# A hand-ordered attention and feed-forward kernel on one core: an earlier bias load, a warm-up on ones and another written-out order

## The chip, the core and the metric

The kernel runs on one core of one Trainium2 chip. The engines of the core run side by side, each through its own queue of instructions in order: TensorE (PE, with its weight loads PEld), VectorE (DVE), ScalarE (ACT), GpSimd (POOL) and SyncE (SP), which here only issues DMAs and passes signals on. DMAs of SP and ACT go over the hardware queues, those of POOL over the software queue. The metric is the device time of one execution in microseconds (us). Three runs of the kernel before took 156.56, 155.41 and 156.89 us; their median is 156.56 us.

## The reference

The input x has 2048 tokens of 448 features, in bf16. It is layer-normed, and the normed xn goes two ways.

```
xn = (x - mean) / sqrt(var + 1e-5)
A: q, k, v = xn @ wqkv, 16 heads of 28
   token s attends to the 8 tokens s, s-2, ..., s-14 (those below 0 are masked)
   s  = softmax(q.k / sqrt(28)) v, heads joined, @ wo
B: h = gelu(xn @ w1 + b1)          (1792 wide)
   g = silu(h @ w2 + b2)
out = x + s * g
```

## The kernel before, in words

Even and odd tokens never attend to each other, so the tokens are sorted into two halves, and 16 tiles of 128 tokens are worked on. For each tile DVE takes the statistics (lines 340 and 344), normalises (line 374) and doubles the last 64 features (line 379), so that the contraction of 448 is three k tiles of 128 rows and one of 64 that is there twice. Tiles 0 to 3 are transposed by PE (line 389) and copied out of PSUM; all later tiles by DMA transposes on SP (line 287).

Most products come as a **pair** (lines 412 to 436): two products run in the upper and lower 64 rows of PE side by side, first part one (4 steps each), then a **hop**, an empty instruction on POOL or SP (line 424) that waits for part one's end and lets part two (3 steps each) start on exchanged rows. The pairs make q, k and v (lines 465 and 489), the first feed-forward product in four chunks of 512 tokens (line 524, with the gelu and the bias b1 in line 528 on ACT), the second one (line 550, 14 and 14 steps) and the output product (line 732). q and k go back through SBUF and SP's DMA transposes to qkT, v through POOL's DMAs (line 281). The attention is 9 blocks of scores (line 650), exp (line 660), mask (line 666), values (line 682) and four DVE steps (lines 692 to 706). Rows that have to change place between the halves are moved by SP's DMAs (lines 627 and 633). The last four tiles use whole products (lines 576 and 747).

Each of the 1044 steps is a task with a number, the engines that it may run on, its dependences and the buffers that it takes and gives back. **ORDER** (lines 17 to 63) is a string that lists all tasks; the letter says the engine: P for PE, V for DVE, A for ACT, G for POOL, S for SP; D is the landing of a DMA. `emit` (line 99) walks through it, so it fixes the order within every queue, and which buffer a task gets: the one of its ring that was given back first. The eight PSUM banks are such a ring.

Tasks that the prediction speaks of, with what they are:

- G17 the identity; G100, G102 and G104 the three masks (one memset and four or six selects each, lines 795 to 802); G50 the memset and G51/D52 the load of b1 as rows (b1r); P190 (line 836) its transpose on PE.
- V1 the memset of the warm-up operand (line 250) and P2 to P14 the 13 warm-up products (line 253).
- P132 to P137 (line 446) the first products of tiles 0 and 1 by k tile, P138 (line 453) their last 64 rows; P122 and P123 the transposes of tile 2, V120 and V121 its normalisation; P128 and P129, V126 and V127 the same of tile 3; V130 the copy of tile 3's transpose.
- P326 and P321 the first feed-forward pairs; they need all of tiles 0 to 3 and the first half of w1.
- P621, hop G622 and P623: the first pair of the second feed-forward product; V627 adds b2 to one of its two results (line 592) and gives back a bank; G280/D281 the load of b2 to all partitions.
- P241 and P234: part one of the pairs that make v of tiles 6 and 7, and q and k of tile 7; P386 the same for tile 10.
- V427 and V428 the normalisation of tile 12, S429/D430 its DMA transpose, P443 part one of its q and k.
- P450, hop 451, P452: q and k of tile 13.
- S232/D233 the transpose of tile 6's q and k, P747 the scores that need them, P374 part one of tile 9's pair and S375/G375 its hop, S441 the transpose of tile 15.
- A54 the load of ACT's table for gelu.

Of the kernel before, what the change touches and what calls it, by code (L numbers as in the profile page):

```python
# [14 lines left out]


ORDER = """
D0 V1 G17 G104 S34 D35 A36 D37 V15 P2 V16 V22 S38 D39 V23 V24 G50 V25 V26 V27 P3 S44 D45 V28 V29 V30 G51 D52 V18 V19
P4 V20 S40 D41 V21 G31 P5 S42 D43 A53 G32 P6 G33 S46 D47 P7 V60 S48 D49 P8 V61 V64 P9 A62 S76 D77 G100 P10 V63 P11
P12 V106 S78 D79 P13 P14 V107 P108 S80 D81 V65 P109 A66 V110 A111 V67 P132 V113 D112 G102 S82 D83 V114 P115 P136  # L20
V117 V68 S86 D87 P116 P133 A118 V69 P190 D119 P137 A70 V71 S88 D89 V120 P134 V121 V72 S90 D91 P122 P123 P135 V73
V191 V124 A74 P138 V75 D125 V126 P149 A139 V127 V140 A143 P128 G150 P129 A148 A54 S141 D142 P151 V130 G168 D169 D131
P326 V153 G170 D171 G172 D173 V101 P163 V84 A145 G327 G174 D175 A152 V96 P328 G178 D179 A144 S154 D155 V85 V97 G176
D177 V94 P156 A329 G164 V95 V92 P321 A330 G99 P165 G322 P341 V200 A167 V204 A166 V205 V201 P323 A325 V93 G342 G157
S202 D203 G98 V192 P331 G332 P343 A324 P158 S206 D207 A344 A345 G180 D181 V196 V193 S194 D195 P333 A334 P346 P316
A159 V197 G182 D183 S198 D199 A335 P336 G317 S272 D273 G337 G347 A160 P318 A319 P348 A350 A349 P227 G228 V298 P338
A340 P229 V230 A339 V302 S276 D277 S278 D279 G252 D253 P222 S274 D275 A320 G280 D281 G223 P536 G537 P224 A231 P538
A539 P526 V304 V305 V225 P546 S146 D147 P215 G184 D185 V300 G527 A540 A226 P516 P528 A529 V301 V299 S232 D233 S161
D162 V303 G306 V351 V363 G547 P548 G517 P518 A530 A519 V103 G290 D291 G216 P217 A218 V359 A520 P521 G522 P541 G542
A550 P523 V355 V356 V219 S357 D358 A524 P531 V313 S220 D221 V307 P543 V364 P208 A549 G186 D187 G532 A545 G286 D287  # L30
V360 P533 A534 G209 P210 A535 A211 A212 A525 A544 A55 V352 P621 P693 V311 A698 A696 S365 D366 A700 V309 V310 G622
P623 V314 V308 V312 G315 V431 A694 S361 D362 V627 V435 P711 A718 A712 P234 G235 V105 V701 V699 P241 A716 G242 V697
V717 G246 D247 S353 D354 P236 S213 D214 G248 D249 P243 G855 A714 V624 G256 D257 A237 P386 V436 V695 P702 V703 V704
S387 P388 A244 G284 D285 A389 A390 A238 V439 V440 G288 D289 V705 G264 D265 G260 D261 V715 V707 V708 A245 G250 D251
V719 P630 G266 D267 G258 D259 S239 D240 V427 G188 D189 V706 V428 S631 S429 D430 P729 A625 A730 A734 V626 P632 A732
G254 D255 V636 S437 D438 V735 A736 A637 V638 G296 D297 V737 G268 D269 V633 P374 G375 P367 S391 D392 G368 P376 A377
P369 P443 A370 G444 A371 S372 D373 V713 V709 P720 V710 V731 A628 V629 P445 A378 V733 A446 A447 G282 D283 P639 V725
V721 V432 A634 S640 V722 S441 D442 V723 V724 V635 S873 D874 P747 A754 A748 V726 V727 V728 S433 D434 P641 V642 S379
D380 V645 P393 G394 A752 G856 S865 D866 P738 V749 G294 D295 P395 V739 V743 V740 P400 S401 A750 P381 G409 D410 G382
A397 P402 V396 G262 D263 V741 V742 S857 D858 P469 V744 G405 D406 G470 S448 D449 S883 D884 P383 A403 V745 A385 S869  # L40
D870 S875 D876 G270 D271 V746 P457 G458 A404 A384 V755 P471 G413 D414 S871 D872 V473 A472 P459 S398 D399 S887 D888
A461 V460 P765 A768 A770 V769 P476 A772 V751 A766 P450 G477 P478 V753 S451 P452 P756 G482 D483 G415 D416 A479 V480
V454 S863 D864 G498 D499 S474 D475 G292 D293 S889 D890 S877 D878 A453 V773 V771 V761 P783 A786 V762 G407 D408 S891
D892 V757 S881 D882 G417 D418 S455 D456 A788 G419 D420 G423 D424 A784 P648 S649 A643 A790 A56 G504 D505 V758 S885
D886 P581 G582 P462 S463 V759 V767 A646 V647 G484 D485 V763 V764 P583 A585 V644 V760 S893 D894 P650 A584 P464 V651
A652 V787 S879 D880 V654 A466 A655 G411 D412 P774 V779 V775 V780 P571 V789 G488 D489 V776 G572 A465 V781 P556 P576
V777 V778 P573 A574 S859 D860 G577 S861 D862 V782 A575 P578 A580 S557 V656 S867 D868 P558 A579 P551 G552 P566 P553
A555 A554 S567 V785 A560 P964 S903 D904 S965 G425 D426 S897 D898 S467 D468 V791 P568 G494 D495 G496 D497 A570 P966
G421 D422 A569 P953 V967 V968 A559 P561 S562 V971 S969 D970 G954 P955 V972 S973 D974 S899 D900 V956 V960 P563 A565
A564 A57 V957 P792 V793 V797 V794 G481 S895 D896 V795 P801 A806 S901 D902 P657 S658 V796 V798 V807 V961 A802 S962  # L50
D963 A808 S911 D912 S905 D906 V653 A804 V805 S907 D908 V799 P819 A822 V803 V800 S913 D914 G490 D491 A824 V825 G500
D501 G486 D487 P659 G492 D493 A826 V809 V660 S915 D916 S909 D910 A661 P810 V811 G510 D511 V815 A820 V663 A664 P666
P837 A840 V816 V817 S667 V812 V813 V814 A838 P668 S919 D920 A844 P986 V818 P975 V665 V672 G514 D515 G502 D503 G987
S923 D924 V662 P988 V989 S976 P977 S929 D930 V993 S958 D959 V990 V669 A842 A58 S925 D926 V994 S991 D992 S931 G506
D507 D932 A670 P591 A673 V982 P586 S587 S921 D922 V978 G592 P593 V841 V823 G508 D509 V821 S917 D918 V979 V827 P596
S597 A594 A595 S927 D928 V839 P588 A590 A589 P598 A600 P616 P828 V833 V834 V835 S617 P618 A599 A619 S980 D981 V836
P611 V983 P1008 A620 V843 S612 P613 P601 A614 V829 V830 V831 S995 D996 S1009 P1010 G602 P603 S984 D985 A615 V832
S933 D934 P997 S998 P606 S607 V674 V1015 A605 V1011 V1016 S1017 D1018 P999 P608 V845 G512 D513 P846 A604 P679 S941
D942 V1012 S1013 D1014 V1000 S939 D940 S937 D938 A609 V847 V851 A610 A59 V848 V852 V849 V853 S935 D936 V850 V854
S943 D944 V671 V1001 S1002 D1003 V1004 S951 D952 S945 D946 S949 D950 S947 D948 V1005 P687 P675 P676 V677 A678 P688  # L60
P1019 P680 V1020 V681 V1021 P1024 S1022 D1023 A682 V1025 V1026 A689 S1006 D1007 S1027 D1028 P683 P684 P1034 V685
A686 P1029 V1035 V1036 S1037 D1038 V1030 P690 P691 V1031 A692 S1032 D1033 P1039 V1040 V1041 S1042 D1043
"""


# [58 lines left out]
def kernel(  # L124
# [106 lines left out]
    plan = _Plan()  # L231
# [11 lines left out]
    def memset(eng, ap, v):  # L243
        def fn(_):
            getattr(nc, eng).memset(ap, v)
        return fn

    warm = p_h.bufs[-1]
    t_on = plan.add("DMA", lambda _: None, ())
    t_warm = plan.add("DVE", memset("vector", warm[:], 0.0), [t_on])  # L250
    for n in (512,) * 8 + (P,) * 5:
        def idle(k, n=n):
            nc.tensor.matmul(buf(p_b, k)[:, :n], warm[:, :P], warm[:, :n], start=True, stop=True)
        t_warm = plan.add("PE", idle, [t_warm], take=(p_b,))
# [669 lines left out]
```

## Time and profile before

| | us |
|---|---|
| runs, median (lowest to highest) | 156.56 (155.41 to 156.89) |
| the profiled execution's own time | 156.29 |
| its span, first to last instruction | 154.5 |
| outside the span | 1.8 |
| PE busy / DVE / ACT / POOL | 147.0 / 105.3 / 89.9 / 45.3 |

The span holds 5764 instructions. In a view, "idle before" is the time that an engine stood still in front of a group, and "<-" names who ended it. The end of a product is modelled, as PE overlaps them; the distance from start to start of two groups is therefore the safer measure of what PE needs for one. A pair's part one on 448 columns takes 0.757 us from start to start, part two 0.567; on 512 columns 0.865 and 0.649. The landing of a DMA is the last of the marks that it leaves on its semaphore.

### The profile page before, as it was taken

To read this page: it belongs to the slowest core of one execution; us is meant where nothing else is said; L and a number is where in the kernel's file an instruction comes from. 1 tells how busy PE (TensorE), PEld (TensorE's weight loads), DVE (VectorE), ACT (ScalarE), POOL (GpSimd) and SP (SyncE) were. 2 spreads that over 40 slices of the span, in tenths; PEclk is the share of its full clock that TensorE was granted. 3 is DMA by queue.
4 is the path that set the end of the run, shared out by engine and by line. 5 is a ranking of instruction groups with operands and counts; after the bars stand their busy time and mean duration, and the time that the engine had idled before them with its cause. 6 is when DMAs were issued, how large, how long until landed. Compare 5 with 4: busy or idle time off the path is not lost.

```text
span 154.5 us, 5764 instructions
## 1 busy us (share of the span) xinstructions
PE 147.0 (95%) x2404; PEld 80.0 (52%) x2404; DVE 105.3 (68%) x271; ACT 89.9 (58%) x167; POOL 45.3 (29%) x100
## 2 busy tenths in 40 slices
PE   6679999999999999899999999999999999999990
PEld 2335555555565555455555445447655565455560
DVE  4967720655503695996978589539987796999462
ACT  3228677847698655634276944696837186660310
POOL 6834650241302495010534821148000110100000
PEclk9999999999999999999999999999999999999999
DMA  5999936999773049642689662055100111121022
GB/s 155 305 286 319 178 92 134 378 290 213 153 75 60 17 110 152 112 98 50 140 158 139 121 75 80 0 129 145 55 17 14 52 55 55 50 71 38 12 89 62
DMA packets 35442, 18.29 MB, mean 118 GB/s; under 512 B 25643, under 2 KB 34263, under 8 KB 35416
## 3 DMA queue, kind: packets, MB, share of 16 engines
q1 hardware_dynamic: 33208, 14.92, 44.2%
q0 software_dynamic: 2064, 2.88, 8.7%
q8 instruction: 19, 0.31, 0.8%
q10 hardware_dynamic: 144, 0.11, 0.3%
q14 instruction: 7, 0.06, 0.2%
HBM read 7.69 MB, written 2.10 MB: 63 GB/s over the span
## 4 chain that ended last, share of the span: by engine, by line
PE 84%; DMA 7%; DVE 4%; POOL 2%; issue 1%; POOLq 0%; DVEq 0%; SPq 0%
PE bank L524 28%; PE bank L550 18%; PE bank L465 11%; PE bank L489 7%; PE bank L576 7%; PE bank L732 5%; PE bank L682 4%; DMA b1r<-in_B_b_dram 4%; DMA xnT<-xn 4%; PE bank L650 3%; PE bank L747 1%; DVE sg L755 1%; DVE dt L692 1%; POOL m L802 0%; POOL m L800 0%
## 5 line engine op out<-in xcount | busy, mean ns | idle before, releaser
L524 PE MATMUL bank<-xnT,w 64*128 64x512 bf16 x392 | 46.3, 376 | 0.0
L281 POOL DMA_DIRECT2D v<-v_tok x52 | 27.4, 533 | 62.5 <-PE bank L732 23.8
L528 ACT ACTIVATE h<-bank,b 128x512 bf16<-128x512 f32 x56 | 35.1, 687 | 16.4 <-PE bank L524 16.1
L550 PE MATMUL bank<-w,h 64*128 64x448 bf16 x336 | 33.9, 349 | 0.0
L524 PEld LDWEIGHTS <-w 64*128 64x128 bf16 x392 | 21.4, 94 | 19.3 <-issue 0.3
L465 PE MATMUL bank<-w_in,xnT 64*128 64x448 bf16 (+1 forms) x212 | 26.6, 350 | 0.9 <-DMA xnT<-xn 0.6
L550 PEld LDWEIGHTS <-h 64*128 64x128 bf16 x336 | 17.0, 94 | 13.1
L660 ACT ACTIVATE E<-bank 128x456 bf16<-128x456 f32 (+1 forms) x36 | 17.0, 552 | 6.1 <-PE bank L650 6.1
L465 PEld LDWEIGHTS <-xnT 64*128 64x128 bf16 (+1 forms) x212 | 10.5, 94 | 10.4 <-DMA xnT<-xn 1.0
L340 DVE BATCH_NORM_STATS2 st<-x_sb 128x6 f32<-128x448 bf16 x16 | 9.5, 612 | 7.8 <-DMA x_sb<-in_A_x_dram 7.8
L592 DVE TENSOR_TENSOR y<-bank,b 128x448 f32<-128x448 f32 x15 | 9.2, 619 | 7.7 <-PE bank L550 6.0
L489 PE MATMUL bank<-w_in,xnT 64*128 64x448 bf16 (+1 forms) x106 | 13.6, 349 | 0.0
L374 DVE TENSOR_SCALAR xn<-x_sb,mv,rstd 128x448 bf16<-128x448 bf16 x16 | 6.2, 408 | 10.8 <-POOL rstd L362 10.7
L692 DVE STREAM_TRANSPOSE dt<-bank 128x480 f32<-128x480 f32 (+1 forms) x18 | 11.4, 659 | 3.0 <-PE bank L682 2.9
L604 ACT ACTIVATE t<-y 128x448 f32<-128x448 f32 x12 | 6.9, 580 | 10.0 <-DVE y L592 10.0
L701 DVE STREAM_TRANSPOSE dt<-rd 128x480 f32<-128x480 f32 (+1 forms) x18 | 11.8, 662 | 0.3
L576 PE MATMUL bank<-w,h 128*128 128x448 bf16 (+2 forms) x70 | 11.4, 315 | 0.0
L706 DVE TENSOR_TENSOR oT<-bank,dt 128x456 bf16<-128x456 f32 (+1 forms) x18 | 11.0, 626 | 0.4
L238 ACT CAST qk_tok<-bank 128x448 bf16<-128x448 f32 x14 | 7.0, 535 | 7.0 <-PE bank L465 6.7
L666 DVE TENSOR_TENSOR E<-E,m_gen 128x456 bf16<-128x456 bf16 x28 | 10.1, 380 | 0.0
L732 PE MATMUL bank<-wo,oT 64*128 64x448 bf16 x42 | 9.2, 349 | 0.0
L732 PE MATMUL bank<-xn,oT 64*128 64x448 bf16 x42 | 9.2, 349 | 0.0
(73 smaller groups left out, 145.0 us busy)
## 6 DMA issues: line engine op xcount, KB each, us to landing
out_dram<-o SPq DMA_DIRECT2D x15, 112.0 KB
w<-in_B_w_dram SPq DMA_DIRECT2D x2, 784.0 KB
w<-in_B_w_dram SPq DMA_DIRECT2D x2, 672.0 KB
x_sb<-in_A_x_dram SPq DMA_DIRECT2D x3, 448.0 KB
v<-v_tok POOLq DMA_DIRECT2D x20, 64.0 KB, 3.1
w_in<-in_A_wqkv_dram SPq DMA_DIRECT2D x3, 336.0 KB
w<-in_B_w_dram SPq DMA_DIRECT2D x4, 112.0 KB
rest<-oT SPq DMA_DIRECT2D x8, 32.0 KB
```

Source lines behind the costliest of these rows:

```text
L281: nc.gpsimd.dma_start(dst(k), src())
L465: return nc.tensor.matmul(ps[:, :D], xnT[r, kt, cs], w, start=start, stop=stop)
L489: return nc.tensor.matmul(ps[:, :D], xnT[r, kt, k0:k0 + P], w, start=start, stop=stop)
L524: return nc.tensor.matmul(ps[:], w1[r, kt, ms], xnT[r, kt, cs], start=start, stop=stop)
L528: nc.scalar.activation(buf(p_h, own, i)[:], buf(p_b, own, i)[:], ACT.Gelu_apprx_tanh, bias=b1[:, mt:mt + 1])
L550: return nc.tensor.matmul(ps[:, :D], buf(*h_at[(c, mt)])[r, j * P:(j + 1) * P], w2[r, mt, :], start=start, stop=stop)
L576: nc.tensor.matmul(ps[:, :n], buf(*h_at[(c, mt)])[:, j * P:(j + 1) * P], w2[:, mt, cs], start=(mt == 0 and not biased), stop=(mt == NMT - 1))
L660: nc.scalar.activation(buf(p_E, k)[:, :n], buf(p_b, a, hl)[:, :n], ACT.Exp, scale=SCALE)
L692: nc.vector.transpose(buf(p_dt, k)[:, :32 * m], buf(p_b, po, i)[:, :32 * m])
L701: nc.vector.transpose(buf(p_dt, d)[:, :32 * m].rearrange("p (b c) -> p b c", c=32), buf(p_rd, r)[:, :m].unsqueeze(2).to_broadcast((P, m, 32)))
L706: nc.vector.tensor_tensor(out=oT[:, :, q0:q0 + 2 * nq], in0=buf(p_b, po, i)[:, :n].rearrange("p (l q) -> p l q", l=4), in1=buf(p_dt, d)[:, ...
L732: return nc.tensor.matmul(ps[:, :D], oT[r, kt, t * P:(t + 1) * P], wo[v][r, kt, :], start=start, stop=stop)
```

## The change

The order string is another one, and the warm-up operand is set to 1.0 in place of 0.0. The number of tasks, their work and their dependences are the same. In the string, PE's tasks stand in the same order up to P151. Behind that they stand in another order: 15 hops go from SP to POOL and 5 from POOL to SP, 14 evacuations from ACT to DVE and 8 from DVE to ACT.

```
-D0 V1 G17 G104 S34 D35 A36 D37 V15 P2 V16 V22 S38 D39 V23 V24 G50 ... G51 D52 ...
+D0 V1 G17 S34 D35 A36 D37 V15 P2 V16 V22 S38 D39 V23 V24 G50 ... G51 D52 ...
...
- ... P151 V130 G168 D169 D131 P326 V153 ... P163 V84 A145 G327 ...
+ ... P151 A152 A153 A54 S154 D155 G178 D179 V130 V144 D131 P321 G174 D175 P326 P163 G327 G322 ... P323 ...
...
- ... S272 D273 ... S276 D277 S278 D279 G252 D253 P222 S274 D275 A320 G280 D281 ... S146 ... S232 ... S161 ...
+ ... S274 D275 ... S272 D273 V298 S278 D279 ... S146 D147 ... S276 D277 ... S161 ...
...
+ ... P541 ... G542 ... P621 ... G172 ... G182 ... G176 D177 G315 ... G296 D297 G280 D281 A698 G622 S213 ...
+ ... P623 V627 ... P711 ... V427 V428 ... P241 S365 ... A628 ... P234 ...
...
-     t_warm = plan.add("DVE", memset("vector", warm[:], 0.0), [t_on])
+     t_warm = plan.add("DVE", memset("vector", warm[:], 1.0), [t_on])
```

G104 stands behind G102 now. V427 and V428 stood on either side of V706, the last of the four DVE steps V703 to V706 of the first attention block's first half; now they stand ahead of V703, and S429, their transpose, ahead of three of the SP tasks that were in front of it. In the old string P234 comes ahead of P241, in the new one behind it. G280, the load of b2, stood ahead of the feed-forward product's second chunk and now stands just ahead of G622. S451 becomes G451, G375 becomes S375, and S232 now stands behind S375 and S441.

More of the change, by code (lines that the diff above doesn't have):

```diff
@@ L17 @@
 ORDER = """
-D0 V1 G17 G104 S34 D35 A36 D37 V15 P2 V16 V22 S38 D39 V23 V24 G50 V25 V26 V27 P3 S44 D45 V28 V29 V30 G51 D52 V18 V19
-P4 V20 S40 D41 V21 G31 P5 S42 D43 A53 G32 P6 G33 S46 D47 P7 V60 S48 D49 P8 V61 V64 P9 A62 S76 D77 G100 P10 V63 P11
-P12 V106 S78 D79 P13 P14 V107 P108 S80 D81 V65 P109 A66 V110 A111 V67 P132 V113 D112 G102 S82 D83 V114 P115 P136
+D0 V1 G17 S34 D35 A36 D37 V15 P2 V16 V22 S38 D39 V23 V24 G50 V25 V26 V27 P3 S44 D45 V28 V29 V30 G51 D52 V18 V19 P4
+V20 S40 D41 V21 G31 P5 S42 D43 A53 G32 P6 G33 S46 D47 P7 V60 S48 D49 P8 V61 V64 P9 A62 S76 D77 G100 P10 V63 P11 P12
@@ L21 @@
+V106 S78 D79 P13 P14 V107 P108 S80 D81 V65 P109 A66 V110 A111 V67 P132 V113 D112 G102 G104 S82 D83 V114 P115 P136
 V117 V68 S86 D87 P116 P133 A118 V69 P190 D119 P137 A70 V71 S88 D89 V120 P134 V121 V72 S90 D91 P122 P123 P135 V73
-V191 V124 A74 P138 V75 D125 V126 P149 A139 V127 V140 A143 P128 G150 P129 A148 A54 S141 D142 P151 V130 G168 D169 D131
-P326 V153 G170 D171 G172 D173 V101 P163 V84 A145 G327 G174 D175 A152 V96 P328 G178 D179 A144 S154 D155 V85 V97 G176
-D177 V94 P156 A329 G164 V95 V92 P321 A330 G99 P165 G322 P341 V200 A167 V204 A166 V205 V201 P323 A325 V93 G342 G157
@@ L25 @@
[L25 to L59, printed above, removed]
@@ L60 @@
-S943 D944 V671 V1001 S1002 D1003 V1004 S951 D952 S945 D946 S949 D950 S947 D948 V1005 P687 P675 P676 V677 A678 P688
-P1019 P680 V1020 V681 V1021 P1024 S1022 D1023 A682 V1025 V1026 A689 S1006 D1007 S1027 D1028 P683 P684 P1034 V685
-A686 P1029 V1035 V1036 S1037 D1038 V1030 P690 P691 V1031 A692 S1032 D1033 P1039 V1040 V1041 S1042 D1043
+V191 V124 A74 P138 V75 D125 V126 P149 A139 V127 V140 A143 P128 G150 P129 A148 S141 D142 P151 A152 A153 A54 S154 D155
+G178 D179 V130 V144 D131 P321 G174 D175 P326 P163 G327 G322 P323 G164 V96 V94 V95 G168 D169 V97 V92 V145 G99 V200
@@ new lines @@
+V204 A325 P328 P165 A166 V201 S202 D203 A330 V205 P341 G342 A324 A329 P336 A167 G337 V84 V85 V93 G98 V192 P343 P338
+A339 A340 S206 D207 V105 P331 V193 S194 D195 V196 A344 V197 G332 P156 S198 D199 S274 D275 V309 G157 S272 D273 V298
+S278 D279 V304 V305 G186 D187 P333 G188 D189 P158 P316 S146 D147 A335 V311 V312 S276 D277 V307 G317 P346 P318 A160
+A159 P227 A345 G347 G184 D185 A319 A334 G228 V308 P348 A350 P229 P526 G527 P546 G252 D253 A320 G547 A349 P528 A529
+V300 S161 D162 A530 P536 G537 A231 P548 A550 V310 P538 P516 G517 P215 G294 D295 A230 A549 P518 A519 G216 P222 G223
@@ new lines @@
+V103 A520 P217 V219 A539 G180 D181 P224 A540 V301 A225 A226 P521 P531 G522 P523 A525 G532 P533 A524 V218 G170 D171
+S220 D221 P208 V302 A535 V303 V299 G306 V101 V359 P541 G209 P210 A211 V351 V363 V364 G542 P543 P621 V360 G172 D173
+S361 D362 A534 A544 V313 V314 V352 G182 D183 P693 A545 A55 V355 V356 S357 D358 G176 D177 G315 V212 V439 A694 V695
+A700 A696 V701 V697 G296 D297 G280 D281 A698 G622 S213 D214 P623 V627 G258 D259 P711 A718 A712 V624 A716 P241 S365
+D366 V427 V428 A714 V699 A628 P234 V719 G242 P386 V435 G235 V713 S353 D354 V715 S429 D430 S387 G256 D257 P702 P236
@@ new lines @@
+V238 A237 P243 V245 P388 V389 A390 P630 G631 G246 D247 A244 G405 D406 S239 D240 A625 V436 V431 P729 S437 D438 G284
+D285 P632 A734 V629 V703 V704 V717 V705 V706 A730 A736 P374 V440 S375 A732 V733 S441 D442 S232 D233 G292 D293 G250
+D251 V737 P443 G444 V735 V633 G264 D265 G266 D267 G248 D249 P376 V731 P445 A447 A634 V626 G855 V378 P367 V707 A377
+P720 V708 V636 A637 G368 V725 V432 A446 V709 V710 G254 D255 V721 P369 A371 S379 A370 D380 V726 V722 V723 V724 P639
+S873 D874 V727 V728 P747 A748 A752 G290 D291 G268 D269 G409 D410 S433 D434 S372 D373 V638 A754 V635 G640 P641 V642
@@ new lines @@
+P400 G401 P393 V645 A646 V753 A750 P738 P402 S391 D392 V739 G260 D261 P381 A404 G382 V740 V403 S394 P395 A396 V741
+V742 V397 G282 D283 P383 A384 G856 G270 D271 V743 V744 G488 D489 V745 V746 P457 S877 D878 G458 S883 D884 A385 P469
+P459 A461 S470 P471 S867 D868 A460 A473 G262 D263 P476 V472 P765 A766 P450 G288 D289 G477 G415 D416 V751 A768 V749
+S871 D872 G413 D414 G451 S861 D862 V755 A772 P478 A480 G419 D420 A770 V479 G286 D287 G407 D408 P452 V453 P756 S891
+D892 S887 D888 P783 V761 V762 V757 A454 V647 A788 A784 V785 G490 D491 A790 S885 D886 G423 D424 A786 A56 V758 P648
@@ new lines @@
+S863 D864 S889 D890 G411 D412 V763 V764 V773 V767 V787 G417 D418 S857 D858 S398 D399 S875 D876 S859 D860 P462 V789
+S869 D870 A643 V644 P581 S463 P464 A466 V769 S881 D882 G492 D493 S865 D866 V759 V465 G649 V760 S893 D894 P650 G582
+P583 A585 P556 V651 A652 A584 P571 S557 P558 A559 G572 P573 P576 G425 D426 S897 D898 G421 D422 V654 V653 A655 V771
+A575 V791 P774 A574 V775 V776 S879 D880 G498 D499 G500 D501 S577 V777 A560 P578 A580 G494 D495 S448 D449 P551 G552
+G482 D483 S455 D456 A579 G504 D505 P566 P553 S899 D900 A555 S901 D902 P964 V779 V656 V780 G484 D485 V781 V782 G965
@@ new lines @@
+S567 P568 P966 G496 D497 A569 V778 A570 P953 G954 V967 P561 G562 V971 V968 P955 P563 P792 V972 G510 D511 S467 D468
+V956 S903 D904 A554 V960 V961 S911 D912 V793 A564 S474 D475 S909 D910 V794 G486 D487 V797 V798 A565 A57 S895 D896
+P801 A804 A802 A806 V795 V796 V803 S969 D970 V805 V807 P657 G658 P819 A822 G512 D513 S905 D906 V799 G502 D503 A820
+V800 S913 D914 A808 V809 V957 P659 V663 V660 A664 G481 A824 S907 D908 V823 A826 P810 V815 S919 D920 S962 V811 D963
+A661 P666 V816 P837 A842 V812 V817 S915 D916 V813 V818 V814 S973 D974 G667 P668 P975 S958 D959 A844 S923 D924 A838
@@ new lines @@
+P986 V843 S987 S921 D922 V662 V672 V665 S927 D928 P591 S929 D930 V669 G976 V825 S925 D926 P988 A840 A58 V827 P977
+V989 V990 V982 G592 S931 D932 A673 V993 P593 A595 P586 V821 A594 S587 S991 D992 V674 S917 D918 V983 V978 V979 G506
+D507 P596 P588 A590 A589 P828 G597 P598 A599 A600 V829 P616 V833 V830 V831 P611 V834 S612 V835 V836 G617 P618 G514
+D515 G508 D509 A619 A620 V832 V845 A670 V994 V839 S984 D985 S933 D934 S941 D942 S935 D936 P1008 G1009 V841 S939 D940
+S980 D981 P613 A614 P1010 P601 P606 G607 V1015 G602 A615 P846 V1011 V1012 P603 A604 S1013 D1014 P997 S937 D938 A605
@@ L63 @@
+P608 A610 V851 G998 P999 V847 V852 V848 V849 V850 V853 V854 S943 D944 V1000 P675 V1016 S995 D996 A609 A59 P676 V671
+V1004 V1005 P687 P688 P679 S1017 D1018 S945 D946 S1006 D1007 V1001 V677 S1002 D1003 P680 A678 P1019 S947 D948 P1024
+P683 P684 S951 D952 S949 D950 P1034 A689 P1029 V681 A682 V1020 V1021 S1022 D1023 P690 P691 V1025 V1026 S1027 D1028
+V685 V1035 P1039 V1036 S1037 D1038 A686 V1030 V1031 S1032 D1033 A692 V1040 V1041 S1042 D1043
 """
```

## The prediction

> **What bounds the kernel.** The page comes first: its busy shares and the chain that ended last.
>
> ```profile
> PE 147.0 (95%) x2404; PEld 80.0 (52%) x2404; DVE 105.3 (68%) x271; ACT 89.9 (58%) x167; POOL 45.3 (29%) x100
> PE 84%; DMA 7%; DVE 4%; POOL 2%; issue 1%; POOLq 0%; DVEq 0%; SPq 0%
> ```
>
> PE is busy for 147.0 of 154.5 us, and the chain is made of PE. A new order removes no product, so it can gain only what PE waits. Where that is, the busy time by stretches of time tells (columns: stretch, its length, busy time of PE, PEld, DVE, ACT, POOL, then granted clock, DMA share, GB/s).
>
> ```profile
> 7.00:10.00 3.00, 2.08 (x15) 1.10 (x15) 2.40 (x8) 0.67 (x2) 1.85 (x8) 1.00 1.07 308
> 30.00:60.00 30.00, 30.00 (x532) 16.60 (x530) 15.71 (x49) 21.29 (x40) 12.82 (x22) 1.00 0.72 144
> 60.00:90.00 30.00, 29.31 (x644) 15.73 (x642) 23.45 (x51) 17.11 (x35) 10.17 (x19) 1.00 0.73 114
> 90.00:120.00 30.00, 30.00 (x646) 16.75 (x642) 24.10 (x53) 19.45 (x35) 6.25 (x13) 1.00 0.25 63
> 120.00:150.00 30.00, 30.00 (x355) 16.39 (x352) 24.02 (x53) 13.67 (x24) 1.56 (x3) 1.00 0.18 54
> ```
>
> From 10 us to 150 us PE stands still for 0.7 us in all, between 60 and 90. So there are three places to gain: the wait before 10 us and two inside 60 to 90. The timeline shows the first (columns: start, length, engine, line, operation, count; idle time before it and who ended it).
>
> ```profile
> 1.32 0.19 POOL L795 MEMSET m<- 128x112 bf16 x1
> ...
> 3.35 0.20 POOL L245 MEMSET b1r<- 128x128 bf16 x1
> ...
> 3.86 0.67 POOL L274 DMA_DIRECT2D b1r<-in_B_b_dram  x1 [0.30 <-POOL b1r L245]
> ...
> 9.48 0.22 PE L836 MATMUL bank<-ident,b1r 128*128 128x128 bf16 x1 [0.92 <-DMA b1r<-in_B_b_dram]
> ...
> 9.54 0.54 PE L465 MATMUL bank<-w_in,xnT 128*128 128x448 bf16 x2
> ```
>
> POOL builds mask G104 from 1.32 us, so b1's rows are issued at 3.86 only; they land 5.49 us later, at 9.35, and P190 keeps PE waiting. The other two waits, from the same view further on:
>
> ```profile
> 57.53 0.38 DVE L374 TENSOR_SCALAR xn<-x_sb,mv,rstd 128x448 bf16<-128x448 bf16 x1
> ...
> 58.57 3.37 SPq L287 DMA_TRANSPOSE xnT<-xn  x2
> ...
> 60.69 2.81 PE L465 MATMUL bank<-w_in,xnT 64*128 64x448 bf16 x28
> ...
> 64.07 0.93 PE L465 MATMUL bank<-w_in,xnT 64*128 64x448 bf16 x8 [0.57 <-DMA xnT<-xn]
> ```
>
> ```profile
> 81.79 0.74 PE L489 MATMUL bank<-w_in,xnT 64*128 64x448 bf16 x6
> 82.65 0.74 PE L465 MATMUL bank<-w_in,xnT 64*128 64x448 bf16 x6
> ```
>
> P443 waits for the transpose of tile 12, which DVE normalised late. P452 starts 0.86 us after a group that needs 0.567: its hop S451 stood in SP's queue behind the moves of rows.
>
> **The change, part by part.** All is counted against the profiled execution: 156.29 us, 0.27 under the median, span 154.5.
>
> *G104 behind G102.* Its memset and six selects fill 1.32 to 3.35, so the memset of b1r and its load come 2.03 us earlier, the load at 1.83. With the same 5.49 us it lands at 7.3; with x's first tile's 2.7 us (0.80 to 3.52) at 4.5. PE can take P190 at 8.40 (P133's start at 7.83 and 0.567), so the wait goes either way. What is late next: P137 needs A118's copy, which ends at 8.41, so it starts at 8.47 in place of 9.54. P134's weights landed at 8.54, it needs them at 9.04. Tile 2's normalised rows are ready at 9.37 and 9.59, PE gets there at 9.61: late by under 0.1. On DVE, V72, V73 and V191 end at 10.39, then V124, V75, V126, V127 (0.42, 0.15, 0.39, 0.18, with hand-overs) end at 11.5; PE reaches tile 3's transposes at 12.0. The first feed-forward pair, at 13.97 now, can start at 12.96; its w1 half landed at 12.6. **Gain 1.0.** The masks end when they did (9.23), as the sum of POOL's work is the same, and their first reader is V101 at 14.63.
>
> *Warm-up on ones.* The memset of zeros took 0.27 as 256 words. At worst it takes twice that, and DVE then idles 1.30 us until x lands, so cover is there; the 13 products start 0.27 later at most, and 0.97 us pass between their end and P108. **0.** Without cover it would be 0.27.
>
> *First products behind P151.* A152, A153 and the table load A54 now follow each other: 13.1 to 15.6 in place of 14.9. The first gelu (A325) waits for P323, whose end is 12.96 + 0.865 + 0.865 + 0.757 + 0.83 = 16.3. Cover 0.7, then 0.
>
> *Tile 12 earlier.* V427 and V428 come right behind V624, near 51 us; S429 follows. With the same 5.45 us it lands near 57, and P443, which 1.89 us of other groups no longer precede, is due near 61. **Gain 0.73** (64.07 less P369's 62.77 and 0.567). What is late next there is tile 6's qkT: S232 now stands behind S375, which waits for P374's end, and S441. From there PE has 5.3 us of work until P747; transposes around there landed in 3.1 to 4.7, this one in 6.2 in its old place. So 0 to 0.9; I take 0.
>
> *Hops and evacuations.* G451 leaves SP's blocked queue: **gain 0.29**. In front of it on POOL are two v loads of 0.52 each, issued before P450 ends; part two of another pair (0.567) covers the rest. 15 hops come to POOL, 5 to SP; a hop caught behind one POOL DMA is 0.5 late, about one covering group. DVE gets 14 casts of 0.62 and gives 8 of 0.54 back: some 109 us of 154.5, still not the bound.
>
> *The tail.* PE's last eight groups and the DVE steps behind them keep their order: from the last product (150.64) to the span's end 3.9 as before.
>
> *The load of b2, moved past much of POOL's queue.* In the new string it follows G542, three v loads, G315 and G296, and G622, V627 follow. The groups of PE ahead of P623 are the same set, so PE's times carry over, 1.0 earlier. P541 starts 2.08 ahead of P621 (42.07 - 2.08 = 39.99) and ends at 41.03; 3 x 0.53 for the v loads, 1.4 for G315, 0.63 for G296: issued at 44.75. P623 ends at 48.3; P234, behind P241, is due at 49.61 and needs the bank that V627 (0.62) gives back. So b2 may take 4.15 us, to 48.9.
>
> ```profile
> wo<-in_A_wo_dram POOLq DMA_DIRECT2D x2, 98.0 KB, 3.5
> ...
> b<-in_B_b_dram POOLq DMA_DIRECT2D x1, 112.0 KB, 6.8
> ```
>
> b2 took 6.8 beside the large loads of x and w2. Those of wo, on the same queue, took 2.5 to 4.6, the 4.6 twice while transposes ran (41.3 and 58.8), and SP runs four transposes here. I take 4.6 as the nearest: **loss 0.5**; bounds 0 (at 2.5) and 2.65 (at 6.8). The Trainium skill, page "DMA: Bandwidth & Descriptors", section "Anatomy of one DMA — SWDGE (gpsimd) path", fits such a load as 2.0 us plus its bytes over 436 GB/s, by which I estimate 2.3 us for b2. By that rule no wait comes and the sum is 154.5; the trace disagrees, no load of wo or b2 landed under 2.5, so the rows decide.
>
> *Small new waits.* Hundreds of neighbourhoods are new; one wait of 0.29 stood in the old order. I put 0.2.
>
> Sum: 156.29 - 1.0 - 0.73 - 0.29 + 0.5 + 0.2 = **155.0 us**, 1.0% under the median.
>
> **Rivals.**
> 1. b2 lands in time (4.15 us or less): 154.5. For it: the large loads are over by 36 us. Against: the 4.6 beside transposes. The Trainium skill's fit, above, points this way.
> 2. b2 is as late as before, 6.8 us: V627 heads DVE's queue and holds P234's bank for 2.65: 154.27 + 2.65 + 0.2 = 157.1, slower than before. It decides from 6.2 us of landing on, where the loss eats all three gains.
> 3. The early load does nothing: the 16 DMA engines are full from 2.5 to 15 us (shares of 0.8 to 1.1), and b1's rows land after 9 us anyway. Then the 1.0 is missing: 156.0. Against: its packets of 256 B ran from 6.6 to 8.1, 2.7 us after the issue, while the large loads ran on.
> 4. Transfers meet elsewhere than I worked out (S232 at 6.2, v loads short of the values, hops behind POOL's DMAs): 1 to 3 us, at 156 to 158.5.
>
> **How the numbers follow.** Chances: forecast 0.45, rival 1 0.17, rival 2 0.13, rival 3 0.10, rival 4 0.15. The runs before spread by 0.9%, so about 1% (1.6 us) is what a measurement can tell from no change. Faster by over 1% is under 155.0: half of the forecast's case and rival 1, 0.40. Slower by over 1% is over 158.1: some of rivals 2 and 4, 0.13. The rest, 0.47, lies within. The range takes in the floor without b2's wait and a little noise below, 153.9, and rivals 2 and 4 up to 157.7.
>
> **What would show it.** Right: P190 and P137 follow P133 with no idle, the first line 524 group starts near 13.0; no idle at P443; line 424's hop before 82 gone; b2's landing in 4 to 5 us and DVE waiting for it at line 592 near 48.5. Wrong: an idle PE over 1 us anywhere between 13 and 148, or PE's first products still at 9.5.

## The result

Over 22 executions of each kernel, the kernel before has a median of 156.81 us (155.41 to 158.24) and the changed one 155.62 us. The ratio is 0.9919, 95% interval 0.989 to 0.9949: 0.8% shorter. The ratio leaves out executions over 1.5% above the fastest of the same kernel: two of the kernel before, and five of the changed one, which took 157.6 to 159.0 us where its other 17 took 154.3 to 156.5. The later sections show a mechanism that makes such a second kind.

The profiled execution of the changed kernel took 155.17 us with a span of 153.4; before it was 156.29 and 154.5. The forecast was 155.0.

The page's busy shares and the chain that ended last, after:

```profile
PE 147.6 (96%) x2404; PEld 79.6 (52%) x2404; DVE 109.5 (71%) x277; ACT 87.0 (57%) x161; POOL 45.5 (30%) x100
PE 85%; DMA 7%; DVE 3%; ACT 1%; SPq 1%; issue 1%
```

PE is still the bound. Three of the stretches of time that were shown of the kernel before, now after (columns as there: stretch, length, busy time of PE, PEld, DVE, ACT, POOL, granted clock, DMA share, GB/s):

```profile
7.00:10.00 3.00, 2.70 (x17) 1.28 (x17) 1.69 (x7) 0.67 (x2) 1.93 (x8) 1.00 1.02 293
60.00:90.00 30.00, 29.83 (x653) 16.21 (x649) 26.74 (x58) 16.36 (x33) 13.18 (x25) 1.00 0.66 114
90.00:120.00 30.00, 29.88 (x641) 16.94 (x639) 23.04 (x50) 19.40 (x35) 6.74 (x13) 1.00 0.43 79
```

From 7 to 10 us PE now stands still for 0.30 in place of 0.92, from 60 to 90 for 0.17 in place of 0.69; from 90 to 120, where there was nothing, 0.12 is new. The front of the timeline after:

```profile
1.82 0.66 POOL L274 DMA_DIRECT2D b1r<-in_B_b_dram  x1 [0.30 <-POOL b1r L245]
...
7.18 0.54 PE L465 MATMUL bank<-w_in,xnT 128*128 128x448 bf16 x2 [0.29 <-DMA w_in<-in_A_wqkv_dram]
...
8.42 0.22 PE L836 MATMUL bank<-ident,b1r 128*128 128x128 bf16 x1
8.48 0.55 PE L465 MATMUL bank<-w_in,xnT 128*128 128x448 bf16 x2
...
9.91 0.31 PEld L389 LDWEIGHTS <-xn 128*128 128x128 bf16 x4 [0.56 <-DVE xn L374]
```

b1's load is issued at 1.82 and lands at 6.89; P190 (line 836) follows without a wait and P137 starts at 8.48, 0.01 from where the prediction put it. That agreement is luck: PE was 0.38 ahead at its first transpose (P108) and lost it again by P133 (7.85, before 7.83). In this execution two other transfers come late: a part of wqkv at 7.18, and x's second pair of tiles, which DVE gets at 8.06 in place of 7.56, so that tile 2's transposes wait at 9.91. The first feed-forward pair starts at 13.28.

The places of the other two gains, in the timeline after:

```profile
60.08 3.57 PE L465 MATMUL bank<-w_in,xnT 64*128 64x448 bf16 x36
```

```profile
80.83 0.73 PE L489 MATMUL bank<-w_in,xnT 64*128 64x448 bf16 x6
81.39 0.73 PE L465 MATMUL bank<-w_in,xnT 64*128 64x448 bf16 x6
```

P443 is inside the first of these lines, at 60.83, with no idle time ahead of it, and P452 starts at 81.39, 0.56 behind the group ahead of it in place of 0.86.

Further on, where the change put b2's load, tile 6's transpose and hop 567 (timeline after):

```profile
45.75 0.59 POOL L274 DMA_DIRECT2D b<-in_B_b_dram  x1
...
49.42 1.16 DVE L592 TENSOR_TENSOR y<-bank,b 128x448 f32<-128x448 f32 x2 [1.53 <-PE bank L650]
50.10 1.69 PE L465 MATMUL bank<-w_in,xnT 64*128 64x448 bf16 x16
...
67.95 0.70 PE L650 MATMUL bank<-qkT 32*64 32x57 bf16 x63 [0.17 <-DMA qkT<-qk_tok]
...
100.42 0.33 PEld L524 LDWEIGHTS <-w 64*128 64x128 bf16 x6 [0.56 <-SPq L424]
```

V627 (line 592) starts at 49.42. The view puts its wait down to PE, but b2 landed at 49.32 and P623 was over at 48.6, so b2 came last. It costs PE 0.18 at P234 (50.10). P747 starts and stops again at 67.95 for tile 6's scores (0.37 from start to start), and part two of pair 568 waits for its hop, which stands behind two moves of rows on SP (0.28).

Start by start, before less after: 0.38 at P108 (x's first tile came 0.15 earlier, and its normalisation took 0.42 in place of 0.65), 0.69 at the first pair, 0.51 behind P234's wait, 1.27 behind P452, 0.72 at the last product; the tail behind that is 3.45 in place of 3.90. Of the 0.69, then, 0.31 was gained behind P108.

### The profile page after: what moved, and what is told of

Same layout as the page of the kernel before. It is cut to its first block, busy times and chain, and to the rows that moved or that the text cites. A ratio compares the mean times of both kernels' runs of the same rounds, so it can differ in the third digit from the quotient of the medians.

```text
span 153.4 us, 5759 instructions
## 1 busy us (share of the span) xinstructions
PE 147.6 (96%) x2404; PEld 79.6 (52%) x2404; DVE 109.5 (71%) x277; ACT 87.0 (57%) x161; POOL 45.5 (30%) x100
## 3 DMA queue, kind: packets, MB, share of 16 engines
q1 hardware_dynamic: 33208, 14.92, 49.4%
## 4 chain that ended last, share of the span: by engine, by line
PE 85%; DMA 7%; DVE 3%; ACT 1%; SPq 1%; issue 1%
PE bank L524 28%; PE bank L550 18%; PE bank L465 11%; PE bank L576 7%; PE bank L489 6%; PE bank L732 5%; PE bank L650 4%; DMA x_sb<-in_A_x_dram 4%; DMA qkT<-qk_tok 4%; PE bank L682 3%; PE bank L747 2%; ACT E L660 1%; SPq L274 1%; DVE E L666 1%; PE bank L389 1%
## 5 line engine op out<-in xcount | busy, mean ns | idle before, releaser
L524 PE MATMUL bank<-xnT,w 64*128 64x512 bf16 x392 | 46.8, 376 | 0.1
L465 PEld LDWEIGHTS <-xnT 64*128 64x128 bf16 (+1 forms) x212 | 11.0, 94 | 10.2 <-issue 1.4
L238 ACT CAST qk_tok<-bank 128x448 bf16<-128x448 f32 x11 | 5.8, 534 | 7.1 <-PE bank L465 7.0
```

Source lines behind the costliest of these rows:

```text
L465: return nc.tensor.matmul(ps[:, :D], xnT[r, kt, cs], w, start=start, stop=stop)
L524: return nc.tensor.matmul(ps[:], w1[r, kt, ms], xnT[r, kt, cs], start=start, stop=stop)
```

## Experiments

All are timed beside the kernel before on the same chip. A "landing" is counted from the issue of the load.

### b1's load alone early

```diff
-G17 G104 S34 D35
+G17 S34 D35
...
-G102 S82 D83
+G102 G104 S82 D83
```

> The kernel before, with one task moved: mask G104 goes behind G102 on GpSimd, so that b1's rows are loaded early. Nothing else. Theory A (the prediction's step): P190 follows P133 without a wait, the first feed-forward pair starts at 12.96 in place of 13.97, and the whole is 1.0 us shorter (0.6%). Theory B (what the trace after the change suggests): the early load goes through the 16 DMA engines while they are full, and x's second pair of tiles lands later for it (8.04 in place of 7.54 there), so that PE waits about 0.3 for the transposes of tile 2; the first pair starts near 13.3 and the whole is 0.7 us shorter. Theory C: the place of the feed-forward's first products comes from the other moves of the new order, and this move alone brings under 0.2.

Measured: 154.94 against 156.07 us, ratio 0.9915 (0.9878 to 0.9951). The timeline of this kernel:

```profile
1.83 0.67 POOL L274 DMA_DIRECT2D b1r<-in_B_b_dram  x1 [0.30 <-POOL b1r L245]
...
8.10 0.22 PE L836 MATMUL bank<-ident,b1r 128*128 128x128 bf16 x1
8.16 0.55 PE L465 MATMUL bank<-w_in,xnT 128*128 128x448 bf16 x2
```

P137 starts 1.38 earlier than before, 0.25 of which were gained ahead of P108. At P621 it is 1.24, so 0.99 net of that: theory A. x's second pair is there at 7.49. It came at 8.05 or later in three of the eight traces with the early load and in one of the six without, so whether the early load can hold it up (theory B) is not settled. This one move gives as much as the whole change.

### Tile 12 alone earlier

```diff
-V624 G256 D257
+V624 V427 V428 G256 D257
...
-S387 P388
+S387 S429 D430 P388
...
-S239 D240 V427 G188 D189 V706 V428 S631 S429 D430 P729
+S239 D240 G188 D189 V706 S631 P729
```

> The kernel before, with tile 12 alone moved: its normalisation on VectorE (V427, V428) right behind V624, and its transpose (S429) behind S387 in SyncE's queue. Theory A (the prediction's step): the normalised rows are ready near 53 in place of 58.5, the transpose lands by 59, P443 has no wait at 64, and the whole is 0.73 us shorter. Theory B: the gain is given back within 20 us, because S429 holds SyncE's queue until V428 is done or VectorE's 0.57 us delay V435's and V439's neighbours, and PE waits for another transpose; the whole is shorter by 0.3 or less.

Measured: 155.84 against 156.07 us, ratio 0.9977 (0.9941 to 1.0013): no difference that can be told, and the 0.73 (0.9953) lies inside the interval. In the trace P443 has no wait, and PE's lead over the kernel before grows there from 0.20 to 0.93; it is 1.09 at the last product. Of the 0.41 that PE led by ahead of the moved steps, 0.20 had gone at P702 (values of the first attention block, at 53.04) and the group behind it. There DVE's last mask product now stands behind its steps for tile 12 and ends 0.15 ahead of P702 in place of 0.59, a cost of the kind that theory B names. So the move is worth 0.53 net here. And the wait that is removed is not a fixed 0.73: in other kernels of this study with tile 12 in its old place it was 0.67 (b1's load alone early), 0.24 (P190 later, below) and nothing (ones alone, below).

### The three moves that the prediction credits

The two edits above, and `S451` becomes `G451`.

> The kernel before, with the three moves that the prediction credits with gains and with nothing else of the new order: G104 behind G102; V427, V428 and S429 earlier; hop 451 on GpSimd in place of SyncE. Theory A (the terms add up as predicted): 1.0 + 0.73 + 0.29 = 2.0 us shorter, profiled near 154.3. Theory B (the front gains only 0.7): 1.7 us shorter, near 154.6, so shorter than the changed kernel's 155.17, because b2's late load and the new small waits (0.18 at tile 7's q and k, 0.37 at tile 6's scores, 0.28 and 0.28 near 96 and 100 us) are not in it. Theory C (the gains need the rest of the new order): less than 1.0 us shorter.

Measured: 154.60 against 156.07 us, ratio 0.9931 (0.9898 to 0.9964). That is 1.1 us, less than theories A (2.0) and B (1.7) say. Up to P792 (103.3 us) the trace has most of it: 2.12 earlier than before, 1.74 net of what came ahead of P108, with 0.75 from the front, as theory B has it. Then 0.68 is lost at one place:

```profile
104.60 2.63 PE L550 MATMUL bank<-w,h 64*128 64x448 bf16 x25
107.64 0.54 PE L550 MATMUL bank<-w,h 64*128 64x448 bf16 x3 [0.41 <-issue]
```

PE pauses inside P657 (a part of the second feed-forward product), whose operands have long been there; "issue" means that the profile knows nobody it waited for. From the start of the 25th product to that of the 26th it is 0.76 here, 0.87 in the run with b1's load alone early, 0.71 in the last experiment below, and 0.08 in the profiled execution of the kernel before. So the terms of the prediction are there in the main, and over a third of them goes to a pause that no step of it had. The last section shows what goes with it.

### Ones alone in the warm-up

```diff
-memset("vector", warm[:], 0.0)
+memset("vector", warm[:], 1.0)
```

> The kernel before, with ones in place of zeros in the warm-up tile. Theory A (the prediction): no difference, within 0.3 us, and P108 starts where it did (5.72). Theory B: products on ones draw more power than products on zeros, and the granted clock falls below 1.0 somewhere; the time is longer by up to 1%. Theory C: the warm-up's memset takes twice as long (0.5 in place of 0.27) and the 13 products start 0.27 later, with no effect behind them.

Measured: 155.67 against 156.07 us, ratio 0.9979 (0.994 to 1.0019), granted clock 1.00: theory A. The memset took 0.48 in place of 0.27 and the products start 0.27 later, with nothing behind them, as theory C has it. What this execution shows besides is of more use. b1's load was issued at 3.86, as in the kernel before, but landed at 7.88 in place of 9.35, and PE did not stand still at all in the stretch that held the prediction's largest term:

```profile
7.00:10.00 3.00, 3.00 (x24) 1.66 (x21) 2.37 (x8) 0.67 (x2) 1.94 (x8) 1.00 0.98 322
```

### The change without the early load

The kernel after with `G104` back behind `G17`.

> The kernel after, with mask G104 back in its old place ahead of b1's load (behind G17); everything else of the change stays. Theory A (the early load is what pays, the rest of the order comes out even): b1 is issued at 3.86 again and lands 4 to 5.5 later, P190 waits up to 1.1 whenever it lands after 8.4; the time is that of the kernel before, ratio 0.997 to 1.003. Theory B (the three places add up as predicted): tile 12's 0.73 and the hop's 0.29 stay, less the waits of 0.18, 0.37, 0.28 and 0.28 that the trace of after shows: 0.1 us gained, ratio 0.999, so the two differ only where the other gains are larger than that. Theory C (the order is what pays, the early load nothing): the ratio stays at 0.992.

Measured: five executions took 155.2 to 156.4 us, and seven 157.6 to 159.2. The ratio of the five is 1.002 (0.9978 to 1.0062), theory A; B's 0.999 lies inside as well, C's 0.992 does not. The median of all twelve is 157.70 against 155.75. The profile is of one of the seven:

```profile
10.10 0.22 PE L836 MATMUL bank<-ident,b1r 128*128 128x128 bf16 x1 [1.72 <-DMA b1r<-in_B_b_dram]
...
52.53 1.16 DVE L592 TENSOR_TENSOR y<-bank,b 128x448 f32<-128x448 f32 x2 [3.37 <-DMA b<-in_B_b_dram]
53.21 1.12 PE L465 MATMUL bank<-w_in,xnT 64*128 64x448 bf16 x10 [1.72 <-DVE y L592]
```

b1 landed after 6.1 us here, and b2, issued at 47.06, after 5.4. So both loads vary from execution to execution, and the rest of the order gains nothing by itself; where b2 lands late, it costs.

### b2 later

```diff
-G280 D281 A698 G622 S213 D214 P623 V627 G258 D259
+A698 G622 S213 D214 P623 G258 D259 G280 D281 V627
```

> The kernel after, with the load of b2 (G280) one v load later in GpSimd's queue: G258 goes ahead of it, so b2 is issued near 46.9 in place of 45.75. Theory A (the prediction's price of a late b2, one for one): b2 lands 1.1 later, near 50.5, V627 ends near 51.1, P234 waits 1.3 in place of 0.18, nothing behind it gives that back, and the whole is 1.1 us longer than the kernel after (ratio against before 0.999 in place of 0.992). Theory B: the work behind P234 is ahead of its own needs; PE finds 0.5 or more of it again at P443 or P747, whose transposes bound it anyway, and the whole is longer by 0.5 or less.

Measured: 157.67 us (155.95 to 158.38) against 155.75, ratio 1.0101 (1.0048 to 1.0154). Slower than before, and by more than either theory said, since the load was issued 0.87 later and took 2.2 longer (5.76 in place of 3.57):

```profile
46.62 0.59 POOL L274 DMA_DIRECT2D b<-in_B_b_dram  x1
...
52.47 1.16 DVE L592 TENSOR_TENSOR y<-bank,b 128x448 f32<-128x448 f32 x2 [4.39 <-DMA b<-in_B_b_dram]
53.15 1.12 PE L465 MATMUL bank<-w_in,xnT 64*128 64x448 bf16 x10 [2.87 <-DVE y L592]
```

P234 waits 3.04 from start to start, 2.86 more than after; at the last product 2.44 are left, 0.19 of it from the front. So the price is nearly one for one: 2.25 of 2.86. Of the 0.61 that was given back, 0.37 is P747's wait, which is not there when PE comes later.

### b2 early, beside the kernel after once more

The kernel after unchanged, and with `G280 D281` right behind `G542`.

> The kernel after, unchanged, beside the next one on the same chip. Theory A (b2's landing decides which group an execution falls into): executions fall into two groups as before, most at 154.3 to 156.5 and about one in four at 157.5 or more, where P234 waits 2 to 3 us for V627 and V627 for b2. Theory B (the group above 157.5 has nothing to do with b2): the same two groups here, and also in the run with b2 early.

> The kernel after, with b2's load alone (G280) right behind hop 542: issued near 41.5 in place of 45.75, so that 6.8 us (the longest landing seen) are covered up to P623's end at 48.3. Theory A (b2's landing decides): no execution above 157, median 0.2 us under the fast group of the kernel after (155.3 to 155.0), P234 follows P241 without a wait. Theory B: about one execution in four stays at 157.5 or more. Theory C (an early b2 pushes the v loads and the rstd of tiles 12 to 15 back by 0.6): PE waits up to 0.6 at P702 or later, and the median is the same or longer.

Measured, in us: unchanged 154.06, 154.52, 154.57, 154.75, 155.21, 155.64, 155.93, 156.55, 157.09, 157.82 and 158.29; with b2 early 154.08, 154.09, 154.14, 154.20, 155.12 and 155.53. The ratios are 0.9922 (0.988 to 0.9963) and 0.9893 (0.9842 to 0.9944). The profile of the unchanged kernel is of the execution of 157.09, and shows where most of the time went:

```profile
45.13 0.59 POOL L274 DMA_DIRECT2D b<-in_B_b_dram  x1
...
50.88 1.16 DVE L592 TENSOR_TENSOR y<-bank,b 128x448 f32<-128x448 f32 x2 [3.74 <-DMA b<-in_B_b_dram]
51.55 1.69 PE L465 MATMUL bank<-w_in,xnT 64*128 64x448 bf16 x16 [2.09 <-DVE y L592]
```

The same kernel and the same load as in the profile above of 155.17, but the landing took 5.65 in place of 3.57, and PE stands for 2.26 from start to start in place of 0.18. With b2 early:

```profile
42.02 0.63 POOL L274 DMA_DIRECT2D b<-in_B_b_dram  x1 [0.98 <-PE bank L465]
...
48.66 1.16 DVE L592 TENSOR_TENSOR y<-bank,b 128x448 f32<-128x448 f32 x2 [0.17 <-PE bank L550]
49.96 1.68 PE L465 MATMUL bank<-w_in,xnT 64*128 64x448 bf16 x16
```

It is issued at 42.02, lands at 45.37, and V627 waits for PE alone. Theory A: with b2 issued behind 45 us, 8 of the 33 executions of this order took over 157 us; with b2 issued near 42 us (this kernel and the two of the next section), none of 20. If nothing but chance stood between them, 20 without one would come about once in 260 times (25/33 to the 20th power). Of the 20, 14 have two more waits mended as well. Beside each other on one chip it is 3 of 11 against none of 12, which chance would give once in about 46 times. The mark of 157 is not b2's alone: the kernel before, whose wait for b1 varies, passes it in 19 of 104 executions, but the four kernels of the old order that lack that wait (b1's load alone early, the three moves, and the last two below) in none of 48.

### Mending the order

The kernel after with three moves: b2 as above; tile 6's transpose ahead of the hop that it stood behind; hop 567 on POOL.

```diff
+G542 G280 D281 P543
...
+S437 D438 S232 D233 G284
...
-S567 P568
+P553 G567 S899
```

> The kernel after, with three of its new waits mended: b2's load (G280) right behind hop 542, three v loads and a rstd earlier; tile 6's transpose (S232) behind S437, ahead of the hop S375 and of S441 in SyncE's queue; hop 567 on GpSimd, right behind P553, in place of SyncE. Theory A (the waits are the cost): P234's 0.18, P747's 0.37 and P568's 0.28 go, 0.8 us in all, profiled near 154.3, ratio against before 0.987. Theory B (another transfer is late right behind): at most 0.3 us shorter than the kernel after, and PE waits at new places.

Measured: 154.30 us (153.90 to 154.56, eight executions) against 155.75, ratio 0.9897 (0.9856 to 0.9938). None of the three waits is left: P234, P747 and P568 follow on. Against the kernel after the last product is 0.98 earlier, 0.45 of which came up to P621, so 0.53 belongs to waits of 0.83. That is nearer to theory A than to B in the trace; the interval holds A's 0.987 and the 0.992 of the kernel after as well.

The same with `P190` behind `P135`:

> The kernel after with the three waits mended (b2 right behind hop 542, tile 6's transpose behind S437, hop 567 on GpSimd) and with P190 behind P135. Theory A (b1's landing is covered by the early load already; P190's place adds nothing but safety): 154.3, as without P190's move. Theory B (b1's landing of 4 to 6 us still costs in some executions): 0.2 us or more under that.

Measured: 154.14 us (153.62 to 155.77, six executions) against 156.46, ratio 0.9882 (0.9822 to 0.9942). P190's place can't be told from nothing (0.9882 beside 0.9897; theory A). The stretches of this kernel:

```profile
7.00:10.00 3.00, 3.00 (x22) 1.60 (x21) 2.00 (x8) 0.67 (x2) 1.93 (x8) 1.00 1.07 315
60.00:90.00 30.00, 30.00 (x658) 16.21 (x654) 27.07 (x58) 16.36 (x33) 13.07 (x25) 1.00 0.55 105
90.00:120.00 30.00, 30.00 (x644) 16.71 (x642) 23.74 (x51) 19.75 (x35) 6.75 (x13) 1.00 0.45 79
```

PE does not stand still in them. These two and the kernel with b2 alone early are 1.0 to 1.2% under the kernel before; their intervals do not tell them apart.

### The other way to take b1's wait out

The kernel before with its late load, and P190 behind P135, where PE comes 2 us later:

```diff
-A118 V69 P190 D119 P137
+A118 V69 D119 P137
...
-P135 V73 V191
+P135 P190 V73 V191
```

> The kernel before, with P190 (the turning of b1's rows) behind P135 in place of ahead of P137; its load stays late (issued at 3.86). Theory A (it is the wait in PE's queue alone that costs): b1 lands by 9.4, PE gets to P190 near 10.5, no wait; P137 starts near 8.4 and the whole is 1.0 us shorter, as with the early load (ratio 0.992 to 0.994). Theory B (the early load brings something besides, for instance that GpSimd's selects no longer run while x is normalised): shorter by 0.5 or less. Theory C: P190's bank is taken and given back later, so that P138 or P149 waits for a bank and half of the gain is lost.

Measured: 155.00 against 155.75 us, ratio 0.9963 (0.9932 to 0.9994). b1 landed at 9.72, after PE would have asked for it in the old place, and no wait came: P137 starts at 8.49, right behind P133. P190 itself:

```profile
10.45 0.22 PE L836 MATMUL bank<-ident,b1r 128*128 128x128 bf16 x1
```

The interval holds A's 0.994 and B's 0.997. The wait in PE's queue goes without any earlier load; whether it is worth the same in time is not settled.

### The old order mended

The kernel before with P190 later, tile 12 earlier and hop 451 on POOL.

> The kernel before, with three moves and its own order otherwise: P190 behind P135, tile 12's normalisation and transpose earlier, hop 451 on GpSimd; b1's load stays late. Theory A (the three terms of the prediction add up on the old order): 1.0 + 0.73 + 0.29 = 2.0 us less, profiled near 154.3, ratio 0.987. Theory B (as with the three moves before: a pause of PE near 108 us, for which the profile names no releaser, takes 0.5 to 0.8 back): ratio 0.992.

Measured: 154.76 against 156.46 us, ratio 0.9904 (0.9872 to 0.9936). Theory B's 0.992 lies inside the interval, theory A's 0.987 at its lower end. In the trace P792 is 1.55 earlier than before, and the pause inside P657 takes 0.62 of it.

## Why the prediction was right, and where it was not

**The sum.** 155.0 was forecast, 155.17 profiled; the ratio times 156.56 makes 155.3. The terms, in the profiled execution, forecast and measured:

| term | forecast | profiled | other executions |
|---|---|---|---|
| PE's start at P108 | 0 | -0.38 | P108 at 5.09 to 5.59 in all 13 others, 5.72 before |
| b1's load early, P108 to the first pair | -1.0 | -0.31 | -0.99 (alone early) |
| tile 12 | -0.73 | -0.73 | wait removed: 0 to 0.73; -0.53 net (alone) |
| hop 451 | -0.29 | -0.29 | |
| b2's load | +0.5 | +0.18 | +2.26 (landing 5.65), +3.04 (issued later, 5.76) |
| tile 6's transpose | 0 | +0.37 | |
| small new waits | +0.2 | +0.28 (hop 567), +0.18 (P774) | 0.2 to 0.9 (hop 567) |
| tail | 0 | -0.44 | 3.45 to 3.46 in the new order, 3.50 to 3.90 in the old |

So part of the agreement is luck. The terms that the prediction counted sum to -1.32 in the forecast and to about -0.3 in this pair of executions. Of the 1.16 that the span lost, 0.38 came from the start, where the profile of the kernel before is the latest of the 14 traces, and 0.44 from the tail, which the prediction held to be unchanged. Why the tail is shorter in every trace of the new order was not followed up. What does not hang on one pair is the ratio of the load alone early, which gives as much as the whole change, and of the change without it, which gives nothing.

**b1.** The step was right: P190 and P137 follow P133, and b1 landed at 6.89, inside the 4.5 to 7.3 given. What it did not say is that the 1.0 depends on the execution. Issued at 3.86, b1 landed after 4.0, 5.5, 5.9 and 6.1 us, and PE waited 0 to 1.9; issued at 1.82, it landed after 3.9 to 5.1 in eight executions, always ahead of PE (8.1 to 8.7). The early load removes a spread, not a constant. In the profiled execution about 0.3 of the gain went to x's second pair, which the prediction did not expect to come later; in five of the eight traces with the early load that pair was not late. Rival 3 is out: the load alone early gave 0.8%.

**Warm-up and table.** Both cost nothing, as forecast: ones alone made no difference that can be told, though the 13 products start 0.27 later, the most that the prediction allowed, and the first gelu at 16.6 is 0.9 behind the end of the table's load. Zeros in the new order were not tried.

**Tile 12 and hop 451.** P443 starts at 60.83 without a wait (forecast: near 61), and the hop's wait before 82 is gone. That V427 and V428 would delay other DVE steps was no term of the sum; in the old order that cost 0.2 at P702 and behind it. Tile 12 alone was worth 0.36 us with an uncertainty of 0.56, which agrees with a wait that is there in some executions only.

**Tile 6's transpose.** The step that it had 5.3 us and would take 3.1 to 4.7 failed in size: issued at 62.41, it landed after 5.5. Its bounds of 0 to 0.9 hold the 0.37.

**Small waits.** I looked at the hops that come to POOL; the one that bit is hop 567, on SP in both orders, with two moves of rows newly ahead of it.

**b2, the step that failed.** I put the issue at 44.75 (its parts add up to 44.65); it came at 45.75 and 45.13, since the v loads ahead of it began 0.6 behind P541's end and not at it, and part of the front's gain was missing. And I took 4.6 us of landing as one number between 2.5 and 6.8. The runs show two kinds instead: 3.4 and 3.6, and 5.4 to 5.8. In the first kind rival 1 is nearly right (0.18 in place of 0), in the second rival 2's mechanism acts at almost its full price (2.26 where the rival has 2.65). The Trainium skill, page "DMA: Bandwidth & Descriptors", section "Anatomy of one DMA — SWDGE (gpsimd) path", gave an estimate of 2.3 us for this load; no run shows less than 3.35. So the two cases were not rivals for one time: both come, by execution. In the profile of the old order this load was issued at 28.6 us, landed at 35.3 and was needed at 49.4, so that no landing seen here could have delayed it.

**What would show it.** P190 and P137 without idle time, P443 without a wait, no wait for the hop before 82, and DVE waiting for b2 at line 592 all came. The first pair is 0.3 later than said, and b2's landing of 3.6 is under the 4 to 5. In the execution of 157.09 a sign of "wrong" came too: PE idle for over 1 us behind 13 us.

## What to carry to other kernels

A wait for a DMA in one profile is one sample of a time that varies. Before you count it as a gain or a loss, look at the same load in several executions, and give its consumer the longest landing that was seen, above all where a change moves its issue from 21 us ahead of need to 3. An edit of a thousand tokens may be worth one of them: put the largest term in alone and time it, and mend the waits that the rest brings one by one. And where a forecast comes out, add up its terms in the trace before you believe them: here the start and the tail, for which the forecast had nothing, gave most of the profiled difference.

## What was not expected of the hardware

- The landing of one load on POOL's queue, of 112 KB, took 3.35 to 5.76 us in six executions of five kernels that issued it between 42 and 47 us. In the execution where it took 5.65, its last packet with payload ended at 48.66, 2.1 ahead of the landing at 50.78; where it took 3.57, at 49.00, 0.3 ahead. So in the first of the two the data were there, and the mark came late, while SP's transposes ran on the same engines (three issued from 44.7 to 48.6 in the one, three from 45.6 to 49.5 in the other). In the landing of 5.76 the data came later too (51.10), and the mark 1.3 behind them. What holds either is open.
- PE paused inside P657, with no releaser in the profile, in four of the seven traces of the old order and two of the seven of the new one: 0.49 to 0.87 from start to start of two products that otherwise follow at 0.08 to 0.13 (0.21 in one more of the old order, counted below as with the pause). Against the kernel before it takes back up to 0.78 us of a lead. It goes with one transfer: in every trace a packet of 16 KB on the DMA queue that the profile lists as "instruction" starts between 0.42 us ahead of P657's start and 0.69 behind it. In the seven traces without the pause this packet ended 0.50 to 1.14 us behind P657's start; in the seven with it, 1.20 to 1.65, and PE went on 1.3 to 1.6 us after its end. That points to a late supply of PE's instructions; no run moved this packet, so it is not shown.
- A granted clock of 0.989 is on record for eight executions, of 157.8 to 159.0 us; all others on record have 0.995 or more. All eight are of kernels that issue b2 behind 45 us. The long time does not need it, as 12 more executions of these kernels are over 157 at 0.997 or more, the three traced ones at 1.0. No trace of 0.989 was kept, so whether the long wait brings the lower clock is open.
